# Block-wise second products of a SwiGLU layer: loads reordered, gate products and stores moved, additions from GpSimd to VectorE

## Chip, cores and metric

One core of a Trainium2 chip runs the whole program. Its engines are named as the profile names them: PE (TensorE), DVE (VectorE), ACT (ScalarE), POOL (GpSimd) and SP (SyncE). The metric is the time of one execution on the device in microseconds; for a kernel it is the median of several runs.

## What is computed

Linear attention over q, k, v gives x (2304 x 512). A mixture of eight experts with soft weights P follows, and then a SwiGLU layer with an RMS norm. The change lies in that last layer:

```python
rms = np.sqrt(np.mean(x * x, axis=-1, keepdims=True) + 1e-06)
xn = x / rms * rms_g
g = xn @ w_gate
silu = g * (1.0 / (1.0 + np.exp(-g)))
val = xn @ w_val
return (silu * val @ w_out).astype(np.float32)
```

Here w_gate and w_val are 512 x 1536 and w_out is 1536 x 512. All products are done in about float32 precision: each operand is split into a high and a low part, and three matmuls (`mm3`, L106 to L109) are added up.

## The kernel before

The 2304 tokens are three groups of 512, 896 and 896 columns (g = 0, 1, 2). A unit u is one slice of 256 columns of the inner dimension for one group. Units 0 to 95 are the mixture of experts (32 a group), units 96 to 113 the SwiGLU layer with six a group, in the order g = 1 (96 to 101), g = 2 (102 to 107), g = 0 (108 to 113). Each unit has a part h (first products) and a part y (second products). The list `order` sets the sequence: units 96 to 107 have h parts alone, and their y work is cut into 14 steps that run between the steps of the next unit's h; units 108 to 113 alternate h and y.

For g = 1 and 2 a first product is done by a Winograd scheme: seven products (`seven`) of weight sums with the block sums of x, B11, T1, B21, T2, B22, T4 and T3 in that order, instead of eight. In units 96 to 107 a pass over the gate weights ("a") is followed by a pass over the value weights ("v"), so h has 14 steps. The block sums live in SBUF (`SX`), one buffer each: those of the next group are loaded from DRAM (`sx_load`) as the last unit's products give each buffer free, in h of 95 for g = 1 and in h of 101 for g = 2. They were written to DRAM before by `norm_steps` (sums of squares, root, scaling, transposes on PE, sums, stores). Weights are loaded a unit ahead by `ws_load` (names wsh and wsl for the two parts, two buffers in turn), those of the second product by `wo_load` (wo_0 to wo_3) or, for g = 0, by `w2_load` (w2r) and split in `w2_split`.

The second product of g = 1 and 2 is block-wise as well: seven products, each with two tiles, are added up over the units in `YM` (`y_steps`). Of the 14 tiles those in `STAGED` are copied from PSUM by ACT and added by POOL; DVE adds the others. When a group is complete, `y_end` combines the seven with seven additions of 128 x 896 and turns the result in 32 x 32 blocks (`y_out`) into staging tiles of four buffers, from which it is stored to `out`.

`hook(i)` runs the tasks of step i. Tasks of one step run as they were registered; `spread` gives out a list of steps over a list of places. This program order is each engine's order, SP's queue of DMA issues included: an issue that waits holds up those behind it. Eight semaphores are given out in turn to all DMAs, so a DMA also waits for the one eight before it.

Of the kernel before, what the change touches and what calls it, by code (L numbers as in the profile page):

```python
# [18 lines left out]
def kernel(  # L19
# [171 lines left out]
    def w2_split(u, f):  # L191
        rv = RAW["b", u]
        if f == 0:
            W2[u] = tuple(
                w2p.tile([P, 2, DM], F32R, tag=f"w2{w}", name=f"w2{w}_{u}") for w in "hl"
            )
        g = group(u)[0]
        if u < NU and g == 2:

            nc.scalar.copy(W2[u][0][:, f], rv[:, f])  # L200
            if f == 0:
                nc.sync.dma_start(
                    W2[u][1].rearrange("p f d -> p (f d)").bitcast(F32), W2D.pop(u)
                )
        else:
            split(W2[u][0][:, f], W2[u][1][:, f], rv[:, f])
        if f == 1:
            if u < NU and g == 1:
                W2D[u + NCH] = dram.tile([P, 2 * DM], F32, tag=f"w2l{u}", name=f"w2d_{u}")
                nc.sync.dma_start(  # L210
                    W2D[u + NCH], W2[u][1].rearrange("p f d -> p (f d)").bitcast(F32)
                )
            del RAW["b", u]
            n = U0 if u + 1 == NU else u + 1
            if n < ALL:
                w2_load(n)

    def ws_alloc(key):
        WS[key] = tuple(
# [878 lines left out]
    def norm_steps(g):  # L1098
# [3 lines left out]
        if g == 0:  # L1102
            return steps + [lambda kk=kk: norm_first(kk) for kk in range(KD)]

        steps += [lambda kk=kk: norm_transpose(g, kk) for kk in range(KD)]
        return steps + sx_all(g + NG, lambda kk, h: norm_place(g, kk, h), True)


    def unit2_h(u, hook):
# [33 lines left out]
        mine = tail_steps(u, cg, cv)  # L1143

        def later(i):
            if i == 7:
                sg.append(gate_sig(flat(cg, 1), 1))
            elif i == 8:
                nc.vector.tensor_tensor(flat(cg, 1), flat(cg, 1), sg[0], op=ALU.mult)
            elif i >= 12:  # L1150
                mine.pop(0)()
            y_step()
            hook(i)

        hook(-1)
        seven(("a", u), cg, later, lambda f: f or gate_part(flat(cg, 0), flat(cg, 0), 0))
        seven(("v", u), cv, lambda i: later(7 + i), lambda f: None)
        assert not YS
        YS.extend(y_steps(u, mine))
# [2 lines left out]
    YM = {}  # L1162
    SB = {}
    WO = {}
    STAGED = (0, 5, 8, 12)
    OT = ["pch", "pcl"]

    def y_step():
# [101 lines left out]

        return [lambda p=p: tile_(p) for p in range(14)]

    def y_out(g, t, j0, n):

        a = YM[g]
        OT.append(OT.pop(0))
        o = decp.tile([P, DM], F32, tag=OT[0], name=f"yout_{g}_{t}_{j0}", bufs=2)
        o = o.rearrange("p (j m b) -> p j m b", m=4, b=32)[:, :n]
        for m in range(4):
# [2 lines left out]
            nc.vector.transpose(  # L1282
                o[:, :, m], src[:, c0:c0 + n * 32].rearrange("p (j b) -> p j b", b=32)
            )
        for j in range(n):
            b, r = divmod(PB0[g] + (j0 + j) * 32, H2)
            jj, p0 = divmod(r, SP)
            rows = out[b * S:(b + 1) * S, :].rearrange("(p c) f -> c p f", c=SC)
            nc.sync.dma_start(
                rows[2 * jj + t, p0:p0 + 32, :].rearrange("a (i x) -> i a x", i=4),  # L1290
                o[:, j].rearrange("p m b -> p (m b)"),
            )

    def y_end(g):

        m = YM[g]
        add = lambda x, y: (lambda: nc.gpsimd.tensor_tensor(m[x], m[x], m[y], op=ALU.add))
        steps = [add(2, 0), add(0, 3), add(4, 1), add(4, 0), add(0, 6), add(5, 0), add(1, 0)]
        return steps + [
            lambda t=t, j=j: y_out(g, t, j, min(4, G // 32 - j))  # L1300
            for t in range(2) for j in range(0, G // 32, 4)
        ]

    def unit2_y(u, hook):
# [66 lines left out]
        TASK.setdefault((kind, u, i), []).append(fn)  # L1371


    for u in range(2, NCH):
        for part in range(2):
            task("y", u - 2, part, lambda u=u, part=part: w1_split(u, part))
# [9 lines left out]
    for u in range(NU, U0):  # L1386
        for i in range(4):
            at = ("h", u, min(4 * i + 3, 13))
            if u == NU:
                at = ("h", u, i) if i < 2 else ("y", u - 1, 6)  # L1390
            task(*at, lambda u=u, i=i: wo_load(u, i))
    for u in range(NCH, 2 * NCH):
        task("h", u - 2, 2, lambda u=u: ws_sums(u))
# [1 line left out]
            task("y", u - 3, i, lambda u=u, i=i: ws_hi(u, i))  # L1395
            task("h", u - 1, -1 if u > NCH else 0, lambda u=u, i=i: ws_lo(u, i))
        task("h", u - 1, 3 if u > NCH else 2, lambda u=u: ws_store(u))

    keys = [("a", u) for u in range(2 * NCH, NU)]
    keys += [(kd, u) for u in range(NU, ALL) for kd in "av"]  # L1400
    for n, key in enumerate(keys):
        if n < 2:
            task("h", key[1] - 2, 6, lambda key=key: ws_load(key))
            continue
        kd, u = keys[n - 2]
        i = 6 if kd == "a" else 13
        if u >= NU and group(u)[0] == 0:
            i = 2 if kd == "a" else 5
        task("h", u, i, lambda key=key: ws_load(key))


    HALVES = [(kd, c, half) for c in range(NC2) for kd in "avo" for half in range(2)]
    LOADED = {}
# [89 lines left out]
    for i in range(7):  # L1503
# [1 line left out]
        task("h", NU + NC2 - 1, 7 + i, lambda i=i: sx_load(NG + 2, i))  # L1505
    spread(
        [("h", u, i) for u in range(NU + 1, NU + NC2)
         for i in (0, 1, 3, 6, 7, 7, 8, 9, 10, 10, 11, 12, 13) if u < NU + NC2 - 1 or i < 5],
        lambda: norm_steps(2),
    )  # L1510
    spread(
        [("h", u, i) for u in range(NU + NC2 + 1, NU + NC2 + 4) for i in (1, 3, 7, 10, 12)],
        lambda: y_end(1),
    )
    task("h", U0 - 1, 0, first_again)
    spread(
        [at for u in range(U0 + 1, U0 + 3)
         for at in [("y", u - 1, i) for i in range(4)] + [("h", u + 1, i) for i in range(6)]],
        lambda: y_end(2),
    )  # L1520
# [208 lines left out]
```

## Time and profile before

| | |
|---|---|
| median of 3 runs | 2045.62 us (2042.52 to 2046.42) |
| profiled execution | 2044.18 us |
| its span, first to last instruction | 2042.4 us |
| PE busy | 1992.6 us (98%) |
| DVE, ACT, POOL busy | 1493.7, 818.9, 560.1 us |
| mean granted clock of PE | 0.993 |

PE is busy throughout but for the last quarter, so the profile is read by stretches: how many matmuls each holds for its length, and what PE waited for there. The units from 96 on begin at about 1582 us, units 102 to 107 at 1747, and unit 108 at 1915.

### The profile page before, as it was taken

To read this page: it belongs to the slowest core of one execution; us is meant where nothing else is said; L and a number is where in the kernel's file an instruction comes from. 1 tells how busy PE (TensorE), PEld (TensorE's weight loads), DVE (VectorE), ACT (ScalarE), POOL (GpSimd) and SP (SyncE) were. 2 spreads that over 40 slices of the span, in tenths; PEclk is the share of its full clock that TensorE was granted. 3 is DMA by queue.
4 is the path that set the end of the run, shared out by engine and by line. 5 is a ranking of instruction groups with operands and counts; after the bars stand their busy time and mean duration, and the time that the engine had idled before them with its cause. 6 is when DMAs were issued, how large, how long until landed. Compare 5 with 4: busy or idle time off the path is not lost.

```text
span 2042.4 us, 26562 instructions
## 1 busy us (share of the span) xinstructions
PE 1992.6 (98%) x9614; PEld 1720.5 (84%) x9614; DVE 1493.7 (73%) x2339; ACT 818.9 (40%) x1501; POOL 560.1 (27%) x476
## 2 busy tenths in 40 slices
PE   7999999999999999999999999999999999899988
PEld 5777888888888888888888888888888889789876
DVE  8885877766777777776568888888855588688753
ACT  5564333354343443343254333343332455344321
POOL 3330000032222222222023332332310146475610
PEclk9999999999999999999999999999999999999998
DMA  8543232365655665554878889888766568857443
GB/s 206 143 128 107 93 104 93 103 221 186 237 208 209 215 226 198 197 204 180 317 269 294 271 288 316 306 311 303 288 236 232 218 222 296 312 202 255 168 167 124
DMA packets 192258, 441.90 MB, mean 216 GB/s; under 512 B 33920, under 2 KB 101504, under 8 KB 191744
## 3 DMA queue, kind: packets, MB, share of 16 engines
q1 hardware_dynamic: 192128, 440.22, 62.6%
q8 instruction: 75, 1.23, 0.3%
q14 instruction: 55, 0.45, 0.1%
HBM read 297.42 MB, written 142.74 MB: 216 GB/s over the span
## 4 chain that ended last, share of the span: by engine, by line
PE 85%; DVE 6%; DMA 4%; ACT 2%; POOL 2%; issue 1%; SPq 0%; DVEq 0%; ACTq 0%; POOLq 0%
PE py L107 13%; PE py L108 12%; PE py L109 12%; PE b_a L109 9%; PE b_a L107 9%; PE b_a L108 9%; PE ph_a L107 3%; PE ph_a L109 3%; PE ph_a L108 3%; DMA sT<-sdT 2%; DVE s L104 1%; PE b_v L107 1%; PE b_v L108 1%; PE b_v L109 1%; PE yo L108 1%
## 5 line engine op out<-in xcount | busy, mean ns | idle before, releaser
L107 PE MATMUL py<-w2h,hh 128*128 128x512 f32 x1152 | 452.6, 393 | 0.7 <-ACT lt L741 0.7
L108 PE MATMUL py<-w2l,hh 128*128 128x512 f32 x1152 | 449.0, 390 | 0.0
L109 PE MATMUL py<-w2h,hl 128*128 128x512 f32 x1152 | 448.6, 389 | 0.0
L863 ACT COPY u_a<-b_a 128x448 f32<-128x448 f32 x228 | 121.6, 533 | 624.7 <-PE b_a L109 601.4
L107 PEld LDWEIGHTS py<-w2h,hh 128*128 128x128 f32 x1152 | 216.2, 188 | 47.1 <-issue 1.5
L109 PEld LDWEIGHTS py<-w2h,hl 128*128 128x128 f32 x1152 | 216.3, 188 | 45.9
L108 PEld LDWEIGHTS py<-w2l,hh 128*128 128x128 f32 x1152 | 216.3, 188 | 43.0
L107 PE MATMUL b_a<-sT,wsh_a 128*128 128x448 f32 x608 | 221.3, 364 | 8.9 <-DMA sT<-sdT 7.3
L109 PE MATMUL b_a<-sT,wsl_a 128*128 128x448 f32 x608 | 221.1, 364 | 0.0
L108 PE MATMUL b_a<-sT,wsh_a 128*128 128x448 f32 x608 | 221.1, 364 | 0.0
L999 DVE SCALAR_TENSOR_TENSOR slot_a<-py,Pm,slot_a 128x512 f32<-128x512 f32 x217 | 162.6, 749 | 52.3 <-PE py L109 50.2
L250 POOL TENSOR_TENSOR sum<-w1r 128x256 f32<-128x256 f32 x32 | 23.8, 742 | 561.5 <-issue 438.1
L999 DVE SCALAR_TENSOR_TENSOR slot_b<-py,Pm,slot_b 128x512 f32<-128x512 f32 x217 | 160.6, 745 | 19.5 <-PE py L109 18.9
L107 PE MATMUL b_a<-sB,wsh_a 128*128 128x448 f32 x456 | 165.5, 363 | 1.7 <-DMA sB<-sdB 1.1
L109 PE MATMUL b_a<-sB,wsl_a 128*128 128x448 f32 x456 | 165.5, 363 | 0.0
L108 PE MATMUL b_a<-sB,wsh_a 128*128 128x448 f32 x456 | 165.3, 363 | 0.0
L887 POOL TENSOR_TENSOR c<-u_a,p_a 128x448 f32<-128x448 f32 x64 | 74.3, 1161 | 327.9 <-ACT u_a L863 327.9
L933 DVE SCALAR_TENSOR_TENSOR hl<-c,hh 128x896 fp32r<-128x896 f32 x128 | 143.5, 1121 | 0.9 <-ACT hh L932 0.7
L104 DVE TENSOR_TENSOR w2l<-w2r,w2h 128x512 fp32r<-128x512 f32 x138 | 107.1, 777 | 49.1 <-ACT w2h L103 49.1
L932 ACT ACTIVATE hh<-c 128x896 fp32r<-128x896 f32 x128 | 122.4, 956 | 29.0 <-POOL c L887 28.2
L107 PEld LDWEIGHTS b_a<-sT,wsh_a 128*128 128x128 f32 x608 | 114.1, 188 | 20.3 <-issue 8.0
L107 PE MATMUL ph_a<-slot_a,wsh_a 128*128 128x512 f32 x304 | 122.0, 401 | 7.5 <-DVE w2l L104 6.3
(278 smaller groups left out, 3913.3 us busy)
## 6 DMA issues: line engine op xcount, KB each, us to landing
w2r<-in_moe_w_dram SPq DMA_DIRECT2D x96, 512.0 KB
w1r<-in_moe_w_dram SPq DMA_DIRECT2D x64, 512.0 KB
wsdh<-wsh_a SPq DMA_DIRECT2D x32, 896.0 KB
wsdl<-wsl_a SPq DMA_DIRECT2D x32, 896.0 KB
wsh_a<-wsdh SPq DMA_DIRECT2D x32, 896.0 KB
wsl_a<-wsdl SPq DMA_DIRECT2D x32, 896.0 KB
wo<-wd_o SPq DMA_DIRECT2D x36, 512.0 KB
w2d<-w2l SPq DMA_DIRECT2D x32, 512.0 KB
```

The lines of the kernel that those rows point to most:

```text
L104: (eng or nc.vector).tensor_tensor(lo, src, hi.bitcast(F32), op=ALU.subtract)
L107: nc.tensor.matmul(ps, lh, rh, start=first, stop=False, skip_group_check=True)
L108: nc.tensor.matmul(ps, lh, rl, start=False, stop=False, skip_group_check=True)
L109: nc.tensor.matmul(ps, ll, rh, start=False, stop=last, skip_group_check=True)
L250: nc.gpsimd.tensor_tensor(s1, a21, a22, op=ALU.add)
L863: nc.scalar.copy(tmp[n], bk[i])
L887: nc.gpsimd.tensor_tensor(c[:, 1, 1], tmp["u3"], tmp["p5"], op=ALU.add)
L932: nc.scalar.activation(th, src, AF.Relu)
L933: return lambda: nc.vector.scalar_tensor_tensor(tl, src, 0.0, th.bitcast(F32), op0=ALU.max, op1=ALU.subtract)
L999: nc.vector.scalar_tensor_tensor(a, py, pe, a, op0=ALU.mult, op1=ALU.add)
```

## The change

- `w2_load` of unit 108 (U0) moves from unit 95 to step 8 of unit 107.
- The `ws_load` tasks are registered ahead of the others, so they come first in their step; two are also moved: v of 96 from step 6 of h of 95 to y of 94, v of 102 from step 13 of h of 101 to step 0 of h of 102. wo_2 and wo_3 of unit 101 move to h of 102.
- The gate's sigmoid and product move: sigmoids at steps 5 and 7, products at steps 7 and 10.
- `STAGED` becomes (2, 4, 12, 13).
- `norm_steps` of g = 2 gets three empty steps ahead of its transposes, and other places.
- `y_end` does its seven additions on DVE, turns two blocks at a time instead of four, and stores a turn one step later. The stores of g = 1 stay on SP's queue, those of g = 2 are issued by ACT. Places are more and later.

```diff
@@ w2_split
-            n = U0 if u + 1 == NU else u + 1
-            if n < ALL:
-                w2_load(n)
+            if u + 1 != NU and u + 1 < ALL:
+                w2_load(u + 1)
@@ norm_steps
+        steps += [lambda: None] * (3 * (g == 2))
         steps += [lambda kk=kk: norm_transpose(g, kk) for kk in range(KD)]
@@ unit2_h
         def later(i):
-            if i == 7:
-                sg.append(gate_sig(flat(cg, 1), 1))
-            elif i == 8:
-                nc.vector.tensor_tensor(flat(cg, 1), flat(cg, 1), sg[0], op=ALU.mult)
+            if i in (5, 7):
+                sg.append(gate_sig(flat(cg, i // 7), i // 7))
+            if i in (7, 10):
+                f = i // 10
+                nc.vector.tensor_tensor(flat(cg, f), flat(cg, f), sg[f], op=ALU.mult)
             elif i >= 12:
                 mine.pop(0)()
...
-        seven(("a", u), cg, later, lambda f: f or gate_part(flat(cg, 0), flat(cg, 0), 0))
+        seven(("a", u), cg, later, lambda f: None)
...
-    STAGED = (0, 5, 8, 12)
+    STAGED = (2, 4, 12, 13)
@@ y_out
-    def y_out(g, t, j0, n):
+    def y_turn(g, t, j0):
...
+        n = min(2, G // 32 - j0)
...
-        for j in range(n):
+        return o
+
+    def y_store(g, t, j0, o):
+
+        for j in range(o.shape[1]):
...
-            nc.sync.dma_start(
+            (nc.sync if g == 1 else nc.scalar).dma_start(
@@ y_end
-        add = lambda x, y: (lambda: nc.gpsimd.tensor_tensor(m[x], m[x], m[y], op=ALU.add))
-        steps = [add(2, 0), add(0, 3), add(4, 1), add(4, 0), add(0, 6), add(5, 0), add(1, 0)]
-        return steps + [
-            lambda t=t, j=j: y_out(g, t, j, min(4, G // 32 - j))
-            for t in range(2) for j in range(0, G // 32, 4)
+        add = lambda x, y: (lambda: nc.vector.tensor_tensor(m[x], m[x], m[y], op=ALU.add))
+        at = [(t, j) for t in range(2) for j in range(0, G // 32, 2)]
+        done = []
+
+        def turn(n):
+            if n:
+                y_store(g, *at[n - 1], done.pop())
+            if n < len(at):
+                done.append(y_turn(g, *at[n]))
+
+        return [add(2, 0), add(0, 3), add(4, 1), add(4, 0), add(0, 6), add(5, 0), add(1, 0)] + [
+            lambda n=n: turn(n) for n in range(len(at) + 1)
         ]
@@ tasks
+    keys = [("a", u) for u in range(2 * NCH, NU)]
+    keys += [(kd, u) for u in range(NU, ALL) for kd in "av"]
+    for n, key in enumerate(keys):
+        if n < 2:
+            task("h", key[1] - 2, 6, lambda key=key: ws_load(key))
+            continue
+        kd, u = keys[n - 2]
+        i = 6 if kd == "a" else 13
+        if u >= NU and group(u)[0] == 0:
+            i = 2 if kd == "a" else 5
+        at = {("v", NU): ("y", NU - 2, 0), ("v", NU + NC2): ("h", NU + NC2, 0)}
+        task(*at.get(key, ("h", u, i)), lambda key=key: ws_load(key))
+
...
+            elif u == NU + NC2 - 1 and i > 1:
+                at = ("h", u + 1, i - 1)
             task(*at, lambda u=u, i=i: wo_load(u, i))
...
-         for i in (0, 1, 3, 6, 7, 7, 8, 9, 10, 10, 11, 12, 13) if u < NU + NC2 - 1 or i < 5],
+         for i in (0, 1, 3, 5, 6, 6, 8, 8, 9, 9, 11, 11, 13) if u < NU + NC2 - 1 or i < 7],
         lambda: norm_steps(2),
...
-        [("h", u, i) for u in range(NU + NC2 + 1, NU + NC2 + 4) for i in (1, 3, 7, 10, 12)],
+        [("h", u, i) for u in range(NU + NC2 + 1, NU + 2 * NC2 - 1) for i in (1, 3, 6, 8, 9, 11)],
         lambda: y_end(1),
...
+    task("h", U0 - 1, 8, lambda: w2_load(U0))
     spread(
-        [at for u in range(U0 + 1, U0 + 3)
+        [at for u in range(U0 + 1, U0 + 4)
          for at in [("y", u - 1, i) for i in range(4)] + [("h", u + 1, i) for i in range(6)]],
```

SP's queue where the block sums of the second group are loaded, in h of unit 101, before (sB and sT are block sums, wo the second product's weights, wsh_v and wsl_v the value weights of unit 102):

```order
L798 DMA sB21_5_16011<-sdB21_5_14688 128x1792
L798 DMA sT2_5_16026<-sdT2_5_14692 128x1792
L1178 DMA wo_101_2_16040<-wd_o_5_13607 128x1024
L798 DMA sB22_5_16042<-sdB22_5_14689 128x1792
L798 DMA sT4_5_16063<-sdT4_5_14693 128x1792
L1178 DMA wo_101_3_16083<-wd_o_5_13607 128x512
L301 DMA wsh_v_102_16085<-wdh_v_0_9627 128x1792
L301 DMA wsl_v_102_16086<-wdl_v_0_9628 128x1792
L798 DMA sT3_5_16089<-sdT3_5_14691 128x1792
```

and now:

```order
L797 DMA sB21_5_16006<-sdB21_5_14686 128x1792
L797 DMA sT2_5_16022<-sdT2_5_14690 128x1792
L797 DMA sB22_5_16036<-sdB22_5_14687 128x1792
L797 DMA sT4_5_16057<-sdT4_5_14691 128x1792
L797 DMA sT3_5_16079<-sdT3_5_14689 128x1792
L300 DMA wsh_v_102_16099<-wdh_v_0_9627 128x1792
L300 DMA wsl_v_102_16100<-wdl_v_0_9628 128x1792
L1179 DMA wo_101_2_16121<-wd_o_5_13607 128x1024
L1179 DMA wo_101_3_16142<-wd_o_5_13607 128x512
```

The last three block sums now stand ahead of the value weights and of wo_2 and wo_3 of unit 101.

SP's queue around h of units 108 and 109, where w2r is the second product's weights before their split, before:

```order
L303 DMA wsh_a_109_17736<-wdh_a_1_10154 128x1024
L303 DMA wsl_a_109_17737<-wdl_a_1_10155 128x1024
L188 DMA w2r_109_17816<-w32_1_10625 128x1024
L303 DMA wsh_v_109_17818<-wdh_v_1_10355 128x1024
L303 DMA wsl_v_109_17819<-wdl_v_1_10356 128x1024
L188 DMA w2r_110_17845<-w32_2_11405 128x1024
```

and now:

```order
L302 DMA wsh_a_109_17766<-wdh_a_1_10154 128x1024
L302 DMA wsl_a_109_17767<-wdl_a_1_10155 128x1024
L302 DMA wsh_v_109_17840<-wdh_v_1_10355 128x1024
L302 DMA wsl_v_109_17841<-wdl_v_1_10356 128x1024
L188 DMA w2r_109_17850<-w32_1_10625 128x1024
L188 DMA w2r_110_17875<-w32_2_11405 128x1024
```

The value weights of unit 109 now stand ahead of its w2r, which waits for the split of unit 108.

SP's queue between the loads of units 111 and 112, with yout the turned output, before:

```order
L303 DMA wsh_v_111_18046<-wdh_v_3_11886 128x1024
L303 DMA wsl_v_111_18047<-wdl_v_3_11887 128x1024
L1289 DMA out_0_dram<-yout_2_0_8_18050 4x32x128 x4
L1289 DMA out_0_dram<-yout_2_0_12_18067 4x32x128 x2
L1289 DMA out_0_dram<-yout_2_1_0_18082 4x32x128 x4
L1289 DMA out_0_dram<-yout_2_1_4_18099 4x32x128 x4
L1289 DMA out_0_dram<-yout_2_1_8_18116 4x32x128 x4
L1289 DMA out_0_dram<-yout_2_1_12_18130 4x32x128 x2
L188 DMA w2r_112_18155<-w32_4_12869 128x1024
L303 DMA wsh_a_112_18173<-wdh_a_4_12409 128x1024
L303 DMA wsl_a_112_18174<-wdl_a_4_12410 128x1024
```

and now:

```order
L302 DMA wsh_v_111_18070<-wdh_v_3_11886 128x1024
L302 DMA wsl_v_111_18071<-wdl_v_3_11887 128x1024
L188 DMA w2r_112_18171<-w32_4_12869 128x1024
L302 DMA wsh_a_112_18196<-wdh_a_4_12409 128x1024
L302 DMA wsl_a_112_18197<-wdl_a_4_12410 128x1024
```

The stores have left this queue. They stand in ACT's order, two DMAs a turn, between its casts, here from h of 110 to h of 111:

```order
L103 CAST hh_110_1_18066<-cg_110_17974 128x512
L1295 DMA out_0_dram<-yout_2_0_2_18047 4x32x128 x2
L1295 DMA out_0_dram<-yout_2_0_4_18076 4x32x128 x2
L1295 DMA out_0_dram<-yout_2_0_6_18091 4x32x128 x2
L1295 DMA out_0_dram<-yout_2_0_8_18106 4x32x128 x2
L1295 DMA out_0_dram<-yout_2_0_10_18121 4x32x128 x2
L103 CAST w2h_111_18142<-w2r_111_17998 128x512
```

ACT casts the second block of unit 110, issues five pairs of stores and then casts the weights of 111.

## Rows read from the trace of the kernel before

**Rows 1.** The page's first part: busy us (share of the span) xinstructions.
```profile
PE 1992.6 (98%) x9614; PEld 1720.5 (84%) x9614; DVE 1493.7 (73%) x2339; ACT 818.9 (40%) x1501; POOL 560.1 (27%) x476
```

**Rows 2.** Busy us (xinstructions) by stretch; then granted clock, DMA share, GB/s.
```profile
1735.00:1770.00 35.00, 27.82 (x124) 24.40 (x123) 22.38 (x31) 12.34 (x24) 15.67 (x12) 0.90 0.88 351
1770.00:1931.00 161.00, 159.63 (x780) 145.69 (x779) 133.51 (x196) 68.08 (x129) 94.58 (x64) 1.00 0.63 221
1931.00:1952.00 21.00, 13.85 (x53) 10.59 (x52) 13.97 (x11) 4.41 (x8) 16.18 (x8) 0.84 0.35 119
1952.00:1989.00 37.00, 37.00 (x165) 30.61 (x165) 19.66 (x55) 10.01 (x17) 0.00 (x0) 1.00 0.48 159
1989.00:2005.00 16.00, 8.90 (x28) 6.38 (x27) 4.43 (x8) 1.72 (x3) 0.00 (x0) 0.68 0.53 183
```

**Rows 3.** Waits of PE, 1560 to 2043: us in total, times, longest.
```profile
PE b_a L107 <- DMA sT<-sdT: 7.3, 2, 5.1
PE ph_v L107 <- DMA wsh_v<-wdh_v: 7.2, 1, 7.2
PE ph_a L107 <- DVE w2l L104: 6.3, 1, 6.3
PE b_v L107 <- DVE cg L886: 2.1, 2, 1.3
PE b_a L107 <- DMA sB<-sdB: 1.1, 1, 1.1
```

**Rows 4.** DMA issues on SyncE's queue around A: start us, us, engine, line, transfer.
```profile
1568.42 0.32 SPq L188 DMA_DIRECT2D w2r<-w  x1
...
1573.69 0.32 SPq L798 DMA_DIRECT2D sT<-sdT  x1
```

**Rows 5.** Stretches of 5 us around A, columns as in rows 2.
```profile
1590.00:1595.00 5.00, 3.25 (x10) 2.95 (x11) 1.71 (x2) 0.59 (x2) 0.57 (x1) 0.75 0.58 196
```

**Rows 6.** Stretches of 5 us around B, columns as in rows 2.
```profile
1745.00:1750.00 5.00, 5.00 (x27) 4.63 (x26) 3.61 (x6) 2.17 (x5) 4.17 (x3) 1.00 1.01 420
```

**Rows 7.** DMA issues on SyncE's queue around B.
```profile
1750.05 0.32 SPq L798 DMA_DIRECT2D sT<-sdT  x1
```

**Rows 8.** Timeline of PE in B: start, us, operation, [idle before it and what ended it].
```profile
1765.21 0.71 PE L107 MATMUL b_a<-sT,wsh_a 128*128 128x448 f32 x1 [5.12 <-DMA sT<-sdT]
```

**Rows 9.** Timelines of GpSimd, VectorE and SyncE's queue in C.
```profile
1935.65 5.01 POOL L1297 TENSOR_TENSOR slot_b<-slot_b 128x896 f32<-128x896 f32 x2
...
1933.64 5.10 DVE L104 TENSOR_TENSOR w2l<-w2r,w2h 128x512 fp32r<-128x512 f32 x2
...
1938.76 0.32 SPq L188 DMA_DIRECT2D w2r<-w  x1
1939.19 0.37 SPq L303 DMA_DIRECT2D wsh_v<-wdh_v  x1
```

**Rows 10.** Instruction groups by form, several stretches: count | busy us, mean ns | idle before.
```profile
L1200 DVE TENSOR_TENSOR cv<-cv,cg 128x896 f32<-128x896 f32 x24 | 27.9, 1163 | 4.8 <-POOL cv L887 4.7
...
L1297 POOL TENSOR_TENSOR slot_b<-slot_b 128x896 f32<-128x896 f32 x4 | 9.6, 2402 | 0.1
...
L1282 DVE STREAM_TRANSPOSE yout<-slot_b 128x128 f32<-128x128 f32 x18 | 4.2, 282 | 5.8 <-DMA out_dram<-yout 5.7
...
L104 DVE TENSOR_TENSOR w2l<-w2r,w2h 128x512 fp32r<-128x512 f32 x4 | 2.7, 673 | 4.5 <-ACT w2h L103 4.5
...
L1282 DVE STREAM_TRANSPOSE yout<-slot_b 128x64 f32<-128x64 f32 x6 | 1.0, 212 | 0.0
```

**Rows 11.** SyncE's queue in D, then pieces of the chain of waits there.
```profile
1973.04 16.37 SPq L1289 DMA_DIRECT2D out_dram<-yout  x20
1989.51 0.55 SPq L188 DMA_DIRECT2D w2r<-w  x1
...
1974.86 6.21 DMA out_dram<-yout
...
1990.63 7.22 DMA wsl_a<-wdl_a
```

More of the change, by code (lines that the diff above doesn't have):

```diff
@@ L1397 @@
         task("h", u - 1, 3 if u > NCH else 2, lambda u=u: ws_store(u))
[L1399 to L1409, printed above, removed]
     HALVES = [(kd, c, half) for c in range(NC2) for kd in "avo" for half in range(2)]
```

## Prediction

> **What bounds the kernel now.** I read the page's first part, then busy time by stretch, then what TensorE (PE) waits for, then the queue of DMA issues and the chain around each wait. PE is busy for 98% of the span [rows 1], so time can only come out of the stretches in which it stands still. The change alters no engine's order ahead of unit 95, whose products begin at 1564 us, so only the last 480 us count. There the stretches differ [rows 2]. From 1770 to 1931 PE issues 780 matmuls in 161 us, 0.206 us each, and from 1952 to 1989 165 wider ones in 37 us, 0.224 us each: these are PE's own pace. Against them stand three bad stretches. 1735 to 1770 holds 124 matmuls, which need 124 x 0.206 = 25.6 of its 35 us: 9.4 us lost (call it B). 1931 to 1952 holds 53, 11.9 of 21 us: 9.1 us lost (C). 1989 to 2005 holds 28, 6.3 of 16 us: 9.7 us lost (D). The waits name the cause [rows 3]: block sums (sT), which end two waits, of 5.1 and 2.2 us; weights of the second products' last group (wsh_v 7.2 us); a wait put down to w2l (6.3 us); and two waits, 2.1 us together, for a VectorE (DVE) addition at L886. The shorter wait for sT, at 1590, is A. After long waits PE also runs slow: in B, C and D the granted clock is 0.90, 0.84 and 0.68 on average [rows 2], which mixes the level of 2.4 GHz with stretches at 1.2 GHz right behind the wait. So a wait removed gives back more than its own length.
>
> **A, the block sums of the first group.** The last of the seven, T3, is issued at 1573.69, behind w2r of unit 108 (1568.42) and both halves of v of unit 96 [rows 4]. The wait for it is the 2.2 us above (7.3 less 5.1). In the slice 1590 to 1595 the clock is 0.75 and ten matmuls take 3.25 us where 2.1 would do [rows 5]; that makes 3.4 us for A. The change puts T3 first. Moved behind it are 0.52 MB (1024 floats in 128 rows) and 1.84 MB (twice 1792 in 128). While DMA is full it moves 420 GB/s [rows 6], so T3 lands 2.36 / 0.42 = 5.6 us sooner, more than the wait. Its v weights then land as the last, 0.52 / 0.42 = 1.2 us before T3 does now; PE, without the 2.2 us of waiting, wants them after the six matmuls of T3's product (1.2 us), so 1.0 us before T3 lands now. It just fits. Gain 3.4 us, bounds 1.5 (v late by 1.9, a landing in doubt by so much) and 3.9 (the slow clock lasts into the next slice).
>
> **B, the block sums of the second group.** T3 is issued at 1750.05 [rows 7], and PE starts its product at 1765.21 after 5.12 us of waiting [rows 8]. DMA is full throughout (share 1.01, [rows 6]), so bytes decide. Moved behind T3 are wo_2 and wo_3 of unit 101 (0.79 MB) and v of unit 102 (1.84 MB): 6.2 us. T3 would land at 1758.9 (some 0.1 before PE starts, less 6.2), and v 4.4 us after it, at 1763.3. PE wanted T3 at 1760.1; freed of a wait of 0.8 us at L886 and of one of 1.1 us for the sum before (sB, [rows 3]), at 1758.2, and v one step later, at 1760.1 (a step is nine matmuls of 0.206, 1.9 us). So about 3.2 us of waiting stay, now mostly on weights: the queue's bytes hardly shrink, they are reordered. Gain 9.4 - 3.2 = 6.2 us. Below, the block sums' stores are now later too: of T4's and T2's, 0.46 MB each, one may fall ahead of the loads (1.1 us), and the wait that is left may again be followed by half clock (2 us): 3.1. Above: 9.4, if the v weights were ahead of my estimate. wo_2 and wo_3, last in this queue, land 1.9 us after v and are wanted a step and more after v's first product, 1.9 us and more: no further wait.
>
> **C, weights for unit 109.** GpSimd (POOL) runs seven additions of 128 x 896 from 1931; two of them take 5.01 us [rows 9]. Beside them VectorE's w2 splits take 5.10 us for two; the same instructions take 0.67 us each in the quiet stretch [rows 10]. SyncE's next load, w2r, waits for those splits until 1938.76, and v's weights stand behind it, at 1939.19 [rows 9]; PE waits 7.2 us for them [rows 3]. The change takes away both: the additions go to VectorE, later, into y of 108 and h of 110, and v's weights stand ahead of w2r in the queue. They can go when unit 108's v products end at 1931, 8 us sooner. What is late next is w2r and a of unit 110, behind the splits of 109.
>
> **D, weights for unit 112.** SyncE issues 28 pieces of output; the last twenty occupy it for 16.37 us from 1973.04, and w2r of 112 follows only at 1989.51, when PE has already run dry; a's last half lands 7.22 us after 1990.63 [rows 11]. The wait put down to w2l is thus one for weights. The stores waited in turn for VectorE, and VectorE for stores that took 6.21 us to land, with four buffers. In the change these 28 are issued by ScalarE (ACT), which is busy for 10 of 37 us ahead of D [rows 2]; at 0.55 us an issue, the longest of this group's single ones [rows 11], they take 15.4 us of its free time. So the weights wait only for their own buffers and for the w2 split. From w2r's issue to a's landing is 8.3 us [rows 11], a unit is 72 x 0.224 = 16.1 us: the split must be done some 8 us into a unit. VectorE, with 14 turns and stores between its splits, may be 2 to 3 us behind. For C and D together I leave 2.6 us of waiting (bounds 0 and 8). Gain 9.1 + 9.7 - 2.6 = 16.2 us.
>
> On this point the row and a rule differ. The row shows a queue that is held up in order, at a DMA share of 0.48 to 0.53 [rows 2], not full engines. The Trainium skill ("DMA: Bandwidth & Descriptors", section "Issuing engines are not separate DMA queues") says that transfers started by different engines run on the same 16 DMA engines and interleave, so that issuing from several saves only the initiating time. By that rule the sum would lose D's gain and end at 2026.9 us; the mechanism is the first rival below.
>
> **Gate products later.** Before, VectorE waits for ScalarE's sigmoid ahead of L886, whose PSUM bank PE wants. Now L886 stands ahead of the product. Gain 2.1 us [rows 3], bounds 0 and 2.5.
>
> **What VectorE takes on.** Fourteen additions, priced by its own of the same size, 1.16 us [rows 10]: 16.3 us, seven in units 103 and 104, seven in the tail. GpSimd loses 14 x 2.4 us [rows 10], and with them the slowing seen in C. Turns of two blocks instead of four: four transposes at 0.21 instead of 0.28 us [rows 10], 14 turns for 8, some 3 us more per group. VectorE is busy for 133.5 of 161 us [rows 2], so two units of 26 us (126 x 0.206) have 8.9 us free, and the seven additions need 8.1. It fits barely; I charge 1.0 us, bounds -1 and 8. The staged additions, (2, 4, 12, 13) for (0, 5, 8, 12), are as many as before, and POOL is busy for 94.6 of 161 us [rows 2]: nothing. w2r of 108, loaded late, is wanted a third into h of 108, more than half a unit after its issue, and DMA is at 0.63 there [rows 2]: nothing. The transposes of the norm, three steps later, keep their number and stand between products as before: nothing.
>
> **Sum.** 3.4 + 6.2 + 16.2 + 2.1 - 1.0 = 26.9 us. The profiled execution took 2044.18 us, 1.4 below the median of 2045.62; from the median, 2045.6 - 26.9 = **2018.7 us**.
>
> **Rivals.**
> Second queue brings only issue time: the transfers stay in each other's way and unit 112's weights come as late as now. D's 8.2 us (9.7 without 1.5, its part of the 2.6 left) are not gained: 2026.9 us. For it: 6.21 us for a small store beside weights. Against it: DMA half idle there. Chance 0.12.
> VectorE becomes the bound: its work in units 103 and 104 goes onto the path, 7 us more than charged, and as much again in the tail: 2025.7 to 2032.7 us. For it: 83% busy. Against it: GpSimd leaves it alone. Chance 0.08.
> Everything is gained: no wait stays in B, C or D, and VectorE costs nothing: 3.4 + 9.4 + 18.8 + 2.1 = 33.7 us, 2011.9 us. Against it: B's bytes. Chance 0.10.
> Slower: ScalarE itself is held by the stores. Fourteen pairs stand in its order between the casts that PE's next products need, over h of 110 to y of 110, about 20 us of PE work. If a pair must land before the next goes, 14 x 6.21 = 87 us. With two in flight it is 43.5 us, 23 us more than the stretch has, and D's gain is gone too: 2018.7 + 23 + 8.2 = 2049.9 us. It decides between two and three in flight (three: 29 us, 9 us over, still faster). Against it: four buffers, and stores one turn behind their transposes. Chance 0.05.
> Gains that cancel against something unseen: 0.03.
>
> **How the numbers follow.** The forecast has 0.62. The range takes in full gain and the first two rivals but for the end of the second: 2010 to 2031 us. A measurement of this kernel can tell 0.2%, 4 us. All cases but the slower one and the cancelled one lie well beyond that: faster 0.92, same 0.03, slower 0.05.
>
> **What would show it.** A: no PE wait for sT near 1590. B: the wait near 1760 names wsh_v or wsl_v instead of sT, and is about 3 us. C: w2l splits near 0.7 us, v of 109 issued near 1931. D: no output on SyncE ahead of w2r of 112, PE without a wait above 2 us from 1950 to the end. Gate: no wait for L886. VectorE: busier, near 24 of 26 us in units 103 and 104, without PE waiting for its PSUM reads. I am wrong if D's stretch still has a wait of over 5 us, if B's wait is not shorter, or if ScalarE shows long waits ahead of its casts after unit 110.

## Result and profile after

The changed kernel takes 2026.8 us (median of 4 runs, 2025.5 to 2027.5) against 2044.7 us for the kernel before in the same series: ratio 0.9912, 95% interval 0.9895 to 0.9929. It is faster by 18 us; the forecast was 27. The profiled execution took 2027.5 us, its span is 2025.7 us, 16.7 us less than before.

The first part of the page of the changed kernel, then busy time by stretch and PE's waits (columns as in [rows 1 to 3]):

```profile
PE 1990.8 (98%) x9614; PEld 1717.1 (85%) x9614; DVE 1507.5 (74%) x2401; ACT 818.8 (40%) x1501; POOL 524.3 (26%) x462
```
```profile
1735.00:1770.00 35.00, 29.17 (x129) 25.97 (x128) 25.16 (x34) 12.21 (x24) 13.55 (x12) 0.90 0.92 360
...
1931.00:1952.00 21.00, 20.86 (x91) 16.62 (x90) 12.49 (x18) 8.13 (x15) 1.96 (x2) 1.00 0.58 201
...
1989.00:2005.00 16.00, 15.24 (x67) 12.31 (x66) 9.51 (x15) 5.25 (x10) 0.00 (x0) 1.00 0.55 180
```
```profile
PE b_a L107 <- DMA sB<-sdB: 4.6, 1, 4.6
PE yo L108 <- DVE s L104: 2.9, 7, 0.7
PE b_v L109 <- DMA wsl_v<-wdl_v: 1.2, 1, 1.2
PE ph_a L109 <- DMA wsl_a<-wdl_a: 0.8, 1, 0.8
...
PE b_v L107 <- DVE cg L885: 0.3, 1, 0.3
```

Against [rows 2, 3]: C holds 91 matmuls where it held 53, D 67 where it held 28. Their waits of 7.2 and 6.3 us are gone. But B, 1735 to 1770, holds 129 where it held 124. It still has a wait for a block sum, now the first of them (sB, B11) and not the last.

Fixed stretches mix things once the work has moved, so I also measure from point to point in PE's timeline: from the first value product of unit 96, right behind A, to the first product of unit 108 (**middle**), and from there to the last matmul (**tail**). The second point, before:

```profile
1911.22 0.40 PE L107 MATMUL ph_a<-slot_a,wsh_a 128*128 128x512 f32 x1
```

and in the changed kernel:

```profile
1911.41 0.40 PE L107 MATMUL ph_a<-slot_a,wsh_a 128*128 128x512 f32 x1
```

Unit 108 begins no sooner than before. The first point stands at 1593.5 before and at 1591.3 after, the last matmul starts at 2037.4 and 2020.7. So A and what lies ahead give 2.3 us, the middle loses 2.4 (317.7 to 320.1), and the tail gives 16.9 (126.2 to 109.3): together the 16.7 of the span. All that the middle should have gained is missing.

SyncE's queue in the changed kernel shows where. First its DMA issues (start us, us, engine, line, transfer), then, from SyncE's waits, one from 1710 to 1775:

```profile
1729.76 0.32 SPq L394 DMA_DIRECT2D sdT<-pch_T  x1
1737.26 0.32 SPq L394 DMA_DIRECT2D sdT<-pcl_T  x1
1737.68 0.38 SPq L300 DMA_DIRECT2D wsh_a<-wdh_a  x1
...
1740.50 0.70 SPq L797 DMA_DIRECT2D sB<-sdB  x1
```
```profile
SPq L394 <- DVE pcl_T L390: 14.9, 3, 7.1
```

The second store of T2 waits 7.1 us for its VectorE split; a of unit 102 and B11 stand behind it. Counted from the first point B11 is issued at 149.2 us here and was at 142.3 us in the kernel before, 6.9 us sooner:

```profile
1735.85 0.61 SPq L798 DMA_DIRECT2D sB<-sdB  x1
```

PE's first product with B11 in the changed kernel starts 11.3 us after that load's issue:

```profile
1751.77 0.74 PE L107 MATMUL b_a<-sB,wsh_a 128*128 128x448 f32 x1 [4.61 <-DMA sB<-sdB]
```

The DMA engines have little to do while the store waits, as the stretch 1730 to 1740 shows (share 0.40). In the 5 us that hold the end of PE's wait the granted clock is 0.61 on average, so PE runs mostly at 1.2 GHz behind it:

```profile
1730.00:1740.00 10.00, 9.61 (x48) 8.72 (x48) 9.05 (x14) 5.11 (x9) 6.35 (x5) 1.00 0.40 117
1750.00:1755.00 5.00, 3.23 (x9) 2.88 (x10) 1.86 (x1) 0.53 (x1) 2.05 (x2) 0.61 1.00 417
```

### The profile page after: what moved, and what is told of

Read it like the earlier page. It is cut to its first block, busy times and chain, and to the rows that moved or that the text cites. A ratio compares the mean times of both kernels' runs of the same rounds, so it can differ in the third digit from the quotient of the medians.

```text
span 2025.7 us, 26651 instructions
## 1 busy us (share of the span) xinstructions
PE 1990.8 (98%) x9614; PEld 1717.1 (85%) x9614; DVE 1507.5 (74%) x2401; ACT 818.8 (40%) x1501; POOL 524.3 (26%) x462
## 4 chain that ended last, share of the span: by engine, by line
PE 86%; DVE 8%; DMA 2%; issue 1%; POOL 1%; ACT 1%; SPq 0%; DVEq 0%; POOLq 0%; ACTq 0%
PE py L107 13%; PE py L108 13%; PE py L109 13%; PE b_a L109 10%; PE b_a L107 9%; PE b_a L108 9%; PE ph_a L107 3%; PE ph_a L109 3%; PE ph_a L108 3%; DVE s L104 2%; DMA wsl_v<-wdl_v 1%; PE px L690 1%; PE yo L108 1%; PE yo L109 1%; PE b_v L109 1%
## 5 line engine op out<-in xcount | busy, mean ns | idle before, releaser
L998 DVE SCALAR_TENSOR_TENSOR slot_b<-py,Pm,slot_b 128x512 f32<-128x512 f32 x217 | 160.5, 745 | 19.6 <-PE py L109 18.9
L104 DVE TENSOR_TENSOR w2l<-w2r,w2h 128x512 fp32r<-128x512 f32 x138 | 99.9, 725 | 46.0 <-ACT w2h L103 46.0
L885 DVE TENSOR_TENSOR c<-b_a,u_a 128x448 f32<-128x448 f32 x64 | 40.0, 624 | 113.9 <-ACT u_a L862 113.9
```

What stands on the lines that cost most here:

```text
L104: (eng or nc.vector).tensor_tensor(lo, src, hi.bitcast(F32), op=ALU.subtract)
L885: nc.vector.tensor_tensor(c[:, 1, 0], bk[2], tmp["u3"], op=ALU.add)
L998: nc.vector.scalar_tensor_tensor(a, py, pe, a, op0=ALU.mult, op1=ALU.add)
```

## Experiments

Each kernel was timed against the kernel before in the same series, so the ratios compare. Middle and tail come from the one profiled run. stores_sp differs from the changed kernel in the tail alone, yet its middle is 1.8 us longer; so a difference of 2 us between two middles shows nothing by itself.

| kernel | median us | ratio, 95% interval | middle | tail |
|---|---|---|---|---|
| before | 2044.7 | 1 | 317.7 | 126.2 |
| changed | 2026.8 | 0.9912 (0.9895 to 0.9929) | 320.1 | 109.3 |
| norm_before | 2019.8 | 0.9876 (0.9861 to 0.9891) | 312.9 | 109.8 |
| no_empty | 2019.6 | 0.9879 (0.9863 to 0.9896) | 313.9 | 109.6 |
| late_stores | 2022.2 | 0.9898 (0.9881 to 0.9915) | 317.4 | 108.4 |
| sums_pool | 2026.9 | 0.9912 (0.9898 to 0.9925) | 321.7 | 108.7 |
| stores_sp | 2027.5 | 0.9914 (0.9901 to 0.9928) | 321.9 | 111.6 |
| old_turns_sp | 2037.3 | 0.9971 (0.9959 to 0.9982) | 321.7 | 118.5 |
| old_turns_act | 2041.6 | 0.9991 (0.9982 to 0.9999) | 321.7 | 122.7 |
| adds_pool | 2033.8 | 0.9952 (0.9940 to 0.9964) | 319.8 | 116.6 |
| loads_back | 2040.3 | 0.9977 (0.9968 to 0.9986) | 327.3 | 113.7 |
| only_loads | 2031.7 | 0.9942 (0.9929 to 0.9954) | 309.8 | 124.1 |
| norm_gate | 2023.2 | 0.9897 (0.9882 to 0.9912) | 316.4 | 109.9 |
| norm_staged | 2016.0 | 0.9866 (0.9851 to 0.9881) | 312.2 | 108.3 |

### The middle: who holds SyncE's queue

**norm_before**, the changed kernel with:

```diff
-        steps += [lambda: None] * (3 * (g == 2))
-         for i in (0, 1, 3, 5, 6, 6, 8, 8, 9, 9, 11, 11, 13) if u < NU + NC2 - 1 or i < 7],
+         for i in (0, 1, 3, 6, 7, 7, 8, 9, 10, 10, 11, 12, 13) if u < NU + NC2 - 1 or i < 5],
```

> The changed kernel with the norm steps of the third group (g = 2) at their old places: no empty steps, stores of T2 and T4 as early in h of 101 as in the kernel before. Theory Q (SyncE's in-order queue was held behind the late stores of T2 and T4, 7 us from 1730 to 1737): the wait of PE for B11 (4.6 us, and half clock behind it) is gone, what is left is a wait of about 3 us for the weights or the last sums, so about 6 us faster than the changed kernel, 2020 to 2022 us. Rival W (bytes: the loads around 1735 to 1765 are more than the DMA engines move, whatever their order): a wait of 4 us or more stays somewhere between 1745 and 1770, 2025 to 2028 us.

SyncE's queue in norm_before:

```profile
1731.92 0.32 SPq L394 DMA_DIRECT2D sdT<-pcl_T  x1
...
1734.37 0.56 SPq L797 DMA_DIRECT2D sB<-sdB  x1
```

and PE's waits there, 1735 to 1770:

```profile
PE b_v L109 <- DMA wsl_v<-wdl_v: 1.5, 1, 1.5
PE b_a L107 <- DMA sT<-sdT: 0.2, 1, 0.2
```

Counted from the first point (1590.6 here) B11 is issued 5.4 us sooner than in the changed kernel, its wait is gone, the middle is 7.2 us shorter. **no_empty** takes out the three empty steps alone (the first line of the diff above):

> The changed kernel without the three empty steps ahead of the norm's transposes, but with the new places. With all of the norm's old timing the first wait of B was gone. Theory Q (what counts is only when T2's and T4's splits leave SyncE's queue free): the steps go three places earlier, no wait of PE for B11 above 0.5 us, 2019 to 2022 us. Rival: the places, not the empty steps, made the stores late, and part of the wait (2 us or more) stays: 2023 to 2026 us.

It does the same within the intervals: the empty steps made the stores late, not the new places.

Both compute the sums earlier as well. Two kernels keep the late steps and change the queue alone. **sums_pool** issues the stores of the third group from GpSimd (q is `nc.gpsimd` for that group):

```diff
-                nc.sync.dma_start(dst(w), cols(t).bitcast(F32))
+                (q or nc.sync).dma_start(dst(w), cols(t).bitcast(F32))
```

> The changed kernel with nothing moved but the queue: the stores of the third group's block sums are issued by GpSimd instead of SyncE; the norm steps stay late. Theory Q (the queue was held): the loads behind these stores go at once, SyncE issues a of 102 and B11 about 3 to 5 us sooner, and the wait for B11 (4.6 us) falls to under 1.5 us: 2021 to 2024 us. Rival L (the late steps themselves: a store that lands late must be loaded again late, whichever queue it is on): B11 gains nothing or the wait moves to T2 or T4, 2025 to 2029 us. If GpSimd's issues hold up its staged additions, slower than 2029 us.

The wait for B11 is gone, but the time is the same. PE's waits there, 1600 to 1770:

```profile
PE yo L108 <- DVE s L104: 4.0, 3, 2.9
PE b_v L107 <- DVE cg L886: 3.0, 2, 2.5
```

Two waits for VectorE have come instead, 2.9 and 2.5 us. GpSimd's and VectorE's timelines ahead of the first, then B11's load and PE's first product with it, in sums_pool:

```profile
1731.58 1.16 POOL L830 TENSOR_TENSOR slot_b<-slot_b 128x448 f32<-128x448 f32 x1
...
1736.03 1.12 POOL L1269 TENSOR_TENSOR slot_a<-yt,slot_a 128x448 f32<-128x448 f32 x1
```
```profile
1732.27 5.36 DVE L104 TENSOR_TENSOR s<-t,s 128x448 fp32r<-128x448 f32 x1 [1.05 <-ACT s L103]
1737.55 0.61 DVE L104 TENSOR_TENSOR s<-cv,s 128x448 fp32r<-128x448 f32 x1
```
```profile
1742.26 0.32 SPq L797 DMA_DIRECT2D sB<-sdB  x1
```
```profile
1752.48 0.36 PE L107 MATMUL b_a<-sB,wsh_a 128*128 128x448 f32 x1
```

GpSimd, late by its waits for the splits, does five additions without a gap; a split that else takes 0.6 us takes 5.36 us beside them and ends half a us after the last. PE stands for it, and so does SyncE: wo_1, next in its queue, waits for a product of PE, and B11 behind it is issued 152.0 us after the first point, later than in the changed kernel (149.2). PE's product with B11 begins at 162.2 us after that point, against 160.5. So the wait for B11 is gone because PE comes later, not because B11 comes sooner. The wait looks as theory Q has it and the time as its rival has it, and the run decides nothing between them. **late_stores** stays on SyncE:

```diff
+                    HELD if g == NG + 2 and j == 1 and nm in ("T2", "T4") else None,
...
+    task("h", NU + NC2 - 1, 9, lambda: [HELD.pop(0)() for _ in range(2)])
```

(`lo` puts its stores into HELD instead of issuing them; the task issues them.)

> The changed kernel, nothing computed earlier, all on the same queue: only the last stores of T2 and T4 (second half of the third group, two parts each) stand later in SyncE's order, behind the loads of B11, T1 and B21 instead of ahead of them. Theory Q (the in-order queue was held by stores that waited for their splits): a of 102 and B11 are issued 3 us or more sooner, the wait of PE for B11 (4.6 us) is under 0.5 us, T2 or T4 may cost up to 2 us in its place: 2019 to 2023 us. Rival L (the splits themselves are too late, so the sums land late in any order): the wait moves to T2 or T4 with 3 us or more, 2024 to 2028 us.

SyncE's queue, SyncE's longest wait for a transfer and PE's first wait in late_stores:

```profile
1734.85 0.43 SPq L804 DMA_DIRECT2D sB<-sdB  x1
...
1749.08 0.32 SPq L804 DMA_DIRECT2D sT<-sdT  x1
```
```profile
SPq L804 <- DMA sdT<-pcl_T: 9.0, 1, 9.0
```
```profile
PE b_a L107 <- DMA sT<-sdT: 2.9, 1, 2.9
```

With the same late splits B11 goes 3.9 us sooner, counted from the first point (1589.6 here), and PE no longer waits for it: the queue was held, as theory Q has it. But T2's load now stands 9.0 us until its own store has landed (a of 102, wo_1 and three block sums were issued just ahead of it, 5.1 MB or 12 us at the 420 GB/s of [rows 6]), and PE waits 2.9 us for T2, close to what rival L has. That is the price of putting T2's store behind those loads; whether its late split alone would cost as much this run does not tell. The middle is 2.7 us shorter than in the changed kernel, and the ratio lower by 0.0014 (2.9 us) with intervals that overlap, so the times alone do not show the gain; B11's issue and the lost wait do. Earlier splits, in norm_before and no_empty, leave no wait above 0.2 us for a block sum.

### The loads

**loads_back** takes the order of loads back, all else as changed; the block that registers `ws_load` stands behind the others again.

```diff
-            if u + 1 != NU and u + 1 < ALL:
-                w2_load(u + 1)
+            n = U0 if u + 1 == NU else u + 1
+            if n < ALL:
+                w2_load(n)
...
-        at = {("v", NU): ("y", NU - 2, 0), ("v", NU + NC2): ("h", NU + NC2, 0)}
-        task(*at.get(key, ("h", u, i)), lambda key=key: ws_load(key))
+        task("h", u, i, lambda key=key: ws_load(key))
...
-            elif u == NU + NC2 - 1 and i > 1:
-                at = ("h", u + 1, i - 1)
...
-    task("h", U0 - 1, 8, lambda: w2_load(U0))
```

> The changed kernel with the loads in the old order: w2r of 108 loaded in h of 95, weights behind the block sums' neighbours as before, v of 96 and v of 102 at their old steps, wo_2 and wo_3 of 101 in h of 101. Theory: A comes back (3.4 us), B loses more than now (its sums land up to 6 us later, on top of 8.8 us lost now; 2 to 5 us more), C comes back only in part (1 to 3 us), since the splits no longer stand beside GpSimd's additions: 2033 to 2038 us. Rival: the order in the queue hardly counts and C's gain was GpSimd's leaving alone: A's 3.4 us only, 2029 to 2031 us.

It is slower than expected: the middle grows by 7.2 us and the tail by 4.4. Of PE's waits there:

```profile
PE b_a L107 <- DMA sT<-sdT: 7.4, 2, 5.2
PE b_a L107 <- DMA sB<-sdB: 4.5, 2, 4.1
PE ph_v L107 <- DMA wsh_v<-wdh_v: 3.3, 1, 3.3
```

B now has both waits, for its first and for its last sum, and C 3.3 of its 7.2 us [rows 3]. **only_loads** is the mirror image: the kernel before with just this reordering, the same lines with + and - exchanged.

> The kernel before with the new order of loads alone (weights after block sums, w2r of 108 in h of 107, v of 96, v of 102, wo_2 and wo_3 of 101 moved); gate, norm, stores and additions as before. Theory: A 3.4, B 7 (its stores are early, so SyncE's queue isn't held) and some 3 to 6 of C's 9.1 are gained, D (9.7) and the gate's 2.1 are not: 13 to 16 us faster than the kernel before, 2028 to 2032 us. Rival: the new order needs the other parts (C's splits still take 5 us for two, D's queue is unchanged) and gains A and B only: 2034 to 2036 us.

Its middle is the shortest of all, 7.9 us less than before: B's waits are down to 1.5 us. But its tail gives only 2.1 us, for the waits there have moved, not gone. From 1900 on:

```profile
PE ph_a L107 <- DVE w2l L104: 5.5, 1, 5.5
PE ph_a L107 <- DMA wsh_a<-wdh_a: 4.1, 1, 4.1
```

C's wait for v of unit 109 has become one of 4.1 us for a of unit 110, and D is as it was. The time, 2031.7 us, is in the theory's range, but C and D together gave 2.1 us, less than the 3 to 6 that it had for C alone, and the middle gave more.

### The tail: additions, turns and the second queue

**adds_pool** changes `y_end`:

```diff
-        add = lambda x, y: (lambda: nc.vector.tensor_tensor(m[x], m[x], m[y], op=ALU.add))
+        add = lambda x, y: (lambda: nc.gpsimd.tensor_tensor(m[x], m[x], m[y], op=ALU.add))
```

> The changed kernel with y_end's fourteen additions of 128 x 896 on GpSimd again, at their new places. Theory (C's slow splits came from these additions, but the weights no longer stand behind the splits, so most of C's gain is the load order's): w2 splits of 2 us and more beside the additions are back, PE waits 1 to 4 us more in the tail, VectorE's slack in units 103 and 104 is not needed: 2027 to 2031 us. Rival V (the additions on VectorE are on the path and cost more than they save): faster, 2022 to 2025 us. Rival G (C is gained by freeing GpSimd, not by the order): a wait of 6 us or more, 2033 us.

VectorE, SyncE's queue and PE's longest wait of the tail in adds_pool:

```profile
1934.49 5.14 DVE L104 TENSOR_TENSOR w2l<-w2r,w2h 128x512 fp32r<-128x512 f32 x2
```
```profile
1939.66 7.64 SPq L188 DMA_DIRECT2D w2r<-w  x2
1947.39 0.38 SPq L302 DMA_DIRECT2D wsh_a<-wdh_a  x1
```
```profile
PE ph_a L107 <- DMA wsh_a<-wdh_a: 4.6, 1, 4.6
```

The slow splits of [rows 9] are back, w2r waits for them, and a of 110 stands behind it. The tail is 7.3 us longer, more than expected: the wait is 4.6 us, and the window from 1952 to 1989 shows a mean clock of 0.92. The time is rival G's, 2033.8 us, with a shorter wait than it named: GpSimd's leaving was worth more than my theory gave it. In the middle, where VectorE takes on the other seven additions, the two kernels differ by 0.4 us, which one profile cannot tell from nothing.

**stores_sp** puts the stores of g = 2 on SyncE again:

```diff
-            (nc.sync if g == 1 else nc.scalar).dma_start(
+            nc.sync.dma_start(
```

> The changed kernel with the 28 stores of the second part of the output (g = 2) on SyncE's queue again, still in pairs and one turn after their transposes. My reading of D (the weights of 111 to 113 stood behind stores that waited): a wait of PE for weights or w2l is back between 1960 and 2010, 4 to 9 us, 2031 to 2036 us. Rival P (pairs and the delay by a turn were enough, the queue is the same 16 engines): no wait over 1 us, 2025 to 2028 us.

The rival P was right, my reading of D fell: the time is that of the changed kernel, and the second queue is worth nothing measurable. SyncE's queue in stores_sp:

```profile
1960.03 11.56 SPq L1295 DMA_DIRECT2D out_dram<-yout  x12
1972.65 0.33 SPq L188 DMA_DIRECT2D w2r<-w  x1
...
1974.24 0.50 SPq L302 DMA_DIRECT2D wsh_a<-wdh_a  x1
```

The stores still take up the queue (12 in 11.56 us), but w2r of 112 stands behind these twelve, with fourteen still to come, and not behind the last. What did that? **old_turns_sp** and **old_turns_act** take back `y_out`: four blocks a step, stored in the same step, and so done in 8 steps instead of 15.

```diff
-            lambda n=n: turn(n) for n in range(len(at) + 1)
+            lambda t=t, j=j: y_out(g, t, j, min(4, G // 32 - j))
+            for t in range(2) for j in range(0, G // 32, 4)
```

> The changed kernel with the output turned four blocks at a time and stored in the same step, on SyncE, as before; additions on VectorE, loads and places as changed. With the stores back on SyncE in pairs the time did not move, so something else in the change took D's wait away. Theory T (turns of two and the store a turn later: no store in the queue waits for its transposes, no transpose for a store): SyncE's stores hold the loads again, PE waits 3 to 9 us between 1960 and 2005, 2030 to 2036 us. Rival O (the order of loads and the later places did it): no wait over 2 us, 2026 to 2028 us.

> The changed kernel with turns of four stored in the same step, but issued by ScalarE. If Theory T holds on SyncE, this tells what the queue alone is worth when the stores do wait: the loads are free of them, so no wait for weights over 1.5 us, 2026 to 2029 us; if ScalarE is held between its casts instead, PE waits for ScalarE or VectorE products of units 110 to 112, 2030 us and more.

SyncE's queue and PE's wait in old_turns_sp:

```profile
1966.01 16.31 SPq L1290 DMA_DIRECT2D out_dram<-yout  x20
1982.42 0.55 SPq L188 DMA_DIRECT2D w2r<-w  x1
```
```profile
PE ph_a L107 <- DVE w2l L104: 5.3, 1, 5.3
```

That is D as before [rows 11]. ScalarE with its queue (ACTq), and PE's wait, in old_turns_act:

```profile
1969.05 11.85 ACTq L1290 DMA_DIRECT2D out_dram<-yout  x18
1980.94 0.62 ACT L103 CAST w2h<-w2r 128x512 fp32r<-128x512 f32 x1 [13.45 <-DMA out_dram<-yout]
```
```profile
PE ph_a L107 <- DVE slot_e L1315: 10.2, 1, 10.2
```

On ScalarE's queue the burst is worse: a cast of w2r waits 13.45 us behind stores, and PE 10.2 us. PE's row names a VectorE addition, but the weights of unit 112 are late too. SyncE's next w2r waits for the split behind that cast, and a of 112 stands behind w2r; its issue on SyncE's queue, and the landing of a's last half in the chain of waits:

```profile
1986.33 0.32 SPq L188 DMA_DIRECT2D w2r<-w  x1
```
```profile
1987.21 7.48 DMA wsl_a<-wdl_a
```

So stores on another queue can still hold up SyncE's loads, through ScalarE's cast. Against the changed kernel the burst costs 12 us on SyncE and 16 us on ScalarE by the ratios (0.0059 and 0.0079 of 2044.7 us), whereas with stores in pairs the queue makes no difference. Whether the smaller turns, the step between turn and store, or the greater number of steps counts most was not tried apart; the queue shows that loads come between the stores when these are spread.

### Gate and staged tiles

Both start from norm_before. **norm_gate**:

```diff
-            if i in (5, 7):
-                sg.append(gate_sig(flat(cg, i // 7), i // 7))
-            if i in (7, 10):
-                f = i // 10
-                nc.vector.tensor_tensor(flat(cg, f), flat(cg, f), sg[f], op=ALU.mult)
+            if i == 7:
+                sg.append(gate_sig(flat(cg, 1), 1))
+            elif i == 8:
+                nc.vector.tensor_tensor(flat(cg, 1), flat(cg, 1), sg[0], op=ALU.mult)
...
-        seven(("a", u), cg, later, lambda f: None)
+        seven(("a", u), cg, later, lambda f: f or gate_part(flat(cg, 0), flat(cg, 0), 0))
```

> The version with the norm's old timing (2019.8 us), and in addition the gate products as before: sigmoid and product of the first half together behind T4's product. My term for the gate was 2.1 us: two waits of PE for the addition at L885 or L886, near 1.3 and 0.8 us, are back, 2021.5 to 2023 us. Rival: VectorE has to do the same work either way and the time is the same, 2019 to 2020.5 us.

PE's waits name it in norm_gate:

```profile
PE b_v L107 <- DVE cg L885: 8.2, 7, 1.5
```

Seven waits against two before. The middle is 3.5 us longer; by the ratios it is 4 us, with intervals that just overlap. With the old staged set the same places show two waits, in the kernel before and in only_loads, so the two seem to go together; those kernels differ from norm_gate in more than the set, and it was not tried alone.

**norm_staged**:

```diff
-    STAGED = (2, 4, 12, 13)
+    STAGED = (0, 5, 8, 12)
```

> The version with the norm's old timing (2019.8 us), and in addition the staged tiles (0, 5, 8, 12) as before. I charged nothing for the new set. In the changed kernel PE waits a dozen times for splits at L104 and L103 from 1630 on, 0.6 to 0.7 us each, that the kernel before hardly has; if the new set causes them, they go: 1 to 2 us faster, 2018 to 2019 us. Rival: they come from the gate's new places or the norm, and nothing changes (2019 to 2020.5 us), or VectorE is later at other tiles and it is slower.

In norm_staged PE waits for a split s twice (1.2 us), in norm_before five times (1.6 us), in the changed kernel seven times (2.9 us). By time the norm's old timing took away more of them than the old set did. Against norm_before the ratio is lower by 0.001, 2 us, less than the intervals can tell. It is the fastest kernel here, 27 us below the kernel before, and its interval (up to 0.9881) ends below that of the changed kernel (from 0.9895). The middle of only_loads with the tail of the changed kernel would be shorter still by 1.4 us as an estimate (309.8 + 109.3 against 312.2 + 108.3), which is less than one profile can tell; it was not tried.

## Why the prediction held, and where it did not

The forecast was faster, 2018.7 us, range 2010 to 2031; measured 2026.8 us. Point by point:

- **A, 3.4 us: right.** No wait is left near 1590. The first value product of 96 begins at 1590.4 us on average over the twelve profiled kernels with the new order, at 1593.9 in the two with the old one.
- **B, 6.2 us: wrong, 1.0 came** (35 us less 129 x 0.206 leaves 8.4 lost, of 9.4). The step that failed is the sentence on the block sums' stores, "now later too", which I priced by their bytes, 1.1 us. They cost as members of an in-order queue: 7.1 us in which SyncE's next loads stood still at a DMA share of 0.40, and B11 issued 6.9 us later than before. The same holds of "The transposes of the norm, three steps later", put at nothing: what follows them three steps later too, down to the split that T2's store waits for, was never followed into SyncE's queue. The rest was sound: in norm_before, with the stores early, the stretch holds 156 matmuls, 2.9 us are lost where I left 3.2, and the wait is for wsl_v, as foretold, if 1.5 us and not 3. The time of norm_before, 2019.8 us, is 1.1 us from the forecast. In the changed kernel one of my signs of being wrong, a wait in B that is not shorter, was nearly met: 4.6 us against 5.1.
- **C and D, 16.2 us: right in size,** 16.9 in the tail. For C the reason holds in both halves: additions back on GpSimd cost 7.3 us of tail, the old load order 4.4. These were each taken from the whole change and do not add up to its gain.
- **D: right for a wrong reason.** I let the second queue free the weights. It does not: with the stores on SyncE the time is the same. The new turns do it: two blocks a step, stored a step later, over more steps, so that loads come between the stores. The price of a store's issue, 0.55 us, was low as well: ten held ScalarE's queue for 9.24 us.
- **Gate, 2.1 us: its waits are gone** (0.3 left), but it is not a gain by itself. PE has other waits for VectorE and ScalarE instead: from 1600 to 1735 its waits add up to 4.2 us, 1.8 before. This was not in the sum. They add up to 3.6 us in norm_before and 3.4 in norm_staged, which has the old staged set too; so neither the norm nor the staged set accounts for them alone, and which part of the change brings the rest was not shown.
- **VectorE, -1.0 us: not contradicted.** In the middle adds_pool and the changed kernel differ by 0.4 us, so VectorE's seven additions cost little there; one profile of each cannot tell 1 us from nothing.

So the sum missed by 9 us: some 5 in B, 2 in the small waits, and the rest below what one profile tells.

The first rival gave 2026.9 us, which is what came, but by luck and another way: it had D unchanged, and D's stretch has no wait above 0.8 us. The rule weighed there, that issuing from several engines saves only initiating time (the Trainium skill, "DMA: Bandwidth & Descriptors", section "Issuing engines are not separate DMA queues"), agrees with stores_sp against the changed kernel (2027.5 and 2026.8 us). But the queue of an engine has a second price that old_turns_sp and old_turns_act show, which is who stands behind a waiting issue. The slower rival, ScalarE held by its stores, is real as a mechanism (13.45 us in old_turns_act); how many stores are in flight, by which I had it decided, was not tried. In the changed kernel itself ScalarE's queue and its casts, then w2r of 112 on SyncE's queue, read:

```profile
1960.90 9.24 ACTq L1295 DMA_DIRECT2D out_dram<-yout  x10
1970.18 0.62 ACT L103 CAST w2h<-w2r 128x512 fp32r<-128x512 f32 x1 [8.67 <-DMA out_dram<-yout]
```
```profile
1973.67 0.32 SPq L188 DMA_DIRECT2D w2r<-w  x1
```

A cast waits 8.67 us. I had called such a wait a sign that I am wrong, and for D's mechanism it is one: w2r of 112 waits for the split behind that cast and goes at 1973.67, no sooner than in stores_sp (1972.65), where the stores stand ahead of it in its own queue. It costs nothing here, since PE does not wait for a of 112 in either kernel.

## What to carry to other kernels

A store moved later is not costed by its bytes. Look at what it waits for and at every load behind it in the same in-order queue; idle DMA engines just ahead of a late load were the sign here. If stores hold up loads, spread them between the loads before giving them another engine's queue, since a burst held up the work behind it on either queue here.

A change of many parts can gain in one stretch what it loses in another: time from point to point in the program, part undone by part, shows it where the total does not. Here the load order alone gained 7.9 us of the middle, the other parts cost it 10.3, and the total showed neither.

## What the runs showed of the hardware that I had not expected

A VectorE split beside GpSimd's additions can take far longer than one of them. Beside additions of 128 x 896 in adds_pool the w2 splits took 2.57 us each (5.14 for two), about as long as one such addition, instead of 0.67 [rows 10]; in sums_pool, beside five additions of 128 x 448 without a gap, one split took 5.36 us. The Trainium skill ("SBUF — State Buffer", section "SBUF: two separate sides") describes a port pair that the two engines share as an exclusive lock for a whole instruction. The first number agrees with that. By a lock of that kind the second would mean that the loser was passed over by several instructions in a row, since the split ended half a us after the last of the five.
